# Mixed score bursts, five attention bursts a group, and two d_ff chunks side by side in a fused attention and feed-forward kernel

## Chip, cores and metric

The kernel runs on one core of a Trainium2 chip. The metric is device time in microseconds; the time shown for a kernel is the median of several runs. Beside these runs there is one profiled execution, from which every row in this text comes.

## What is computed

Two attention results are added and fed to a two-layer network (8 batches, 8 heads, 576 positions, 64 per head; model width 512, d_ff 2048):

```python
q_d = q.reshape(B, H, Sd, 4, D).mean(axis=3)          # and k_d, v_d: Sd = 144
out_d = softmax(scale * q_d @ k_d.T) @ v_d            # "down" attention
out_up = np.repeat(out_d, 4, axis=2)
mask = np.abs(pos[:, None] - pos[None, :]) < 4        # "local" attention
out_local = softmax(where(mask, scale * q @ k.T, -1e9)) @ v
x = (out_up + out_local).transpose(0, 2, 1, 3).reshape(4608, 512)
h = x @ w_in
return (h / (1 + exp(-1.702 * h))) @ w_out            # float32
```

## The kernel before

**Feed-forward.** The 4608 tokens are cut into 9 groups of 512. For a group, `mm1` forms 16 chunks of d_ff (128 rows each, four matmuls of 128x512 that accumulate over the model width, L691), and ScalarE's SiLU (L702) turns each chunk into one slice of `gT`. Then `mm2` multiplies `gT` by `w_out` for four blocks of 128 tokens, 16 matmuls each (L747), and a ScalarE copy and a DMA store each block (L732). Group g's first product needs `xT`, the attention result of batches g and g-1 (a batch has 576 tokens), with one tile `xT[hp]` for each pair of heads; matmul dmc of a chunk reads `xT[dmc]`.

**Attention is woven in by position.** While group g's dense matmuls run, the attention of batch g+1 is computed in short bursts between them. The order is written by hand: all engines run in the order in which the code issues to them. A position below 16 stands before that chunk of `mm1`; a position from 16 stands before matmul (position - 16) of `mm2`. `POS` is for groups 1 to 6, `POS_0` for group 0; groups 7 and 8 have no attention. The steps of `attention` in groups 1 to 6, with their old positions:

- 13: scores of the first four heads, `s_pe(0)`. `scores` issues 80 local matmuls (L367; 32 rows by 64 columns of the array, 60 columns streamed, ordered by segment i, half of the contraction a, column half par, row strip r). `scores_d` then issues 24 down matmuls (L386; 144 columns streamed).
- 16: `s_act(0)`: ScalarE loads the exponential's table and takes two local exponentials (L397) and the down one (L403); VectorE multiplies by the mask (L411).
- 33: the same for the other four heads, and the SiLU table is loaded again (L661).
- 42: attention times values of head pairs 0 and 1 (80 matmuls, L428 and L450); VectorE normalises (L466, L467).
- 53: the same for pairs 2 and 3.
- 62: transposes of pairs 0 and 1 (26 matmuls each, L481 and L491); ScalarE copies the down part fourfold (L605), VectorE adds it to the local part into `xT` (the merge, L626 and L632).
- 71: the same for pairs 2 and 3.

Group 0 has nine steps (its transposes one by one), with its bank pairs chosen by hand, and 14 further matmuls at 41 (L329) that reduce v.

**PSUM.** Eight banks: three pairs `PA[0..2]`, which attention takes in turn (`ps_tile`), and two single banks `PM`, which the chunks of `mm1` and the blocks of `mm2` take alternately. A score step takes three pairs (two local, one down), an attention step two, a transpose one. A matmul that writes into a bank waits until the last reader has finished. In group 0 the token blocks 2 and 3 (from position 32) go to `PA[0]`.

**Beside it**, at a group's start, VectorE transposes the next batch's q and k (L262), GpSimd reduces them and v (L292, L296, L308, L311) and issues loads, and SP issues loads of v and the stores.

Of the kernel before, what the change touches and what calls it, by code (L numbers as in the profile page):

```python
# [19 lines left out]
def kernel(  # L20
# [9 lines left out]
    nc = tc.nc  # L30
    B, H, S, D = q.shape
    SD = S // 4
# [3 lines left out]
    n_dmc = d_model // 128  # L36
# [3 lines left out]
    KSTART = (0, 56)  # L40
    QSTART = (0, 60)
# [314 lines left out]
    def scores(b, qd, barred=False, sp=None):  # L356
        sp = sp or [ps_tile(), ps_tile()]
        if barred:
            bar_others(sp)
        for i in range(5):  # L360
            for a in range(2):
                for par in range(2):
                    for r in range(4):
                        rows = slice(32 * r, 32 * r + 32)
                        k0 = 114 * i + KSTART[par]
                        q0 = 114 * i + QSTART[par]
                        nc.tensor.matmul(  # L367
                            sp[r // 2][64 * par : 64 * par + 64, r % 2, 60 * i : 60 * i + 60],
                            lhsT=kT[b, qd][rows, k0 : k0 + 64, a],
                            rhs=qT[b, qd][rows, q0 : q0 + 60, a],  # L370
                            start=(a == 0 and not barred),
                            stop=(a == 1 or barred),
                            tile_position=(32 * r, 64 * par),
                            skip_group_check=barred,
                        )
        return sp

    def scores_d(b, qd, sd=None):
        sd = sd or ps_tile()
        bank = banks(sd)  # L380
        for kc in range(3):
            for a in range(2):
                for r in range(4):
                    rows = slice(32 * r, 32 * r + 32)
                    j = r % 2
                    nc.tensor.matmul(  # L386
                        bank[r // 2][64 * j : 64 * j + 64, SD * kc : SD * kc + SD],
                        lhsT=kdT[qd][rows, 48 * kc : 48 * kc + 64, a],
                        rhs=qdT[b, qd][rows, :, a],
                        start=(a == 0), stop=(a == 1),  # L390
                        tile_position=(32 * r, 64 * j),
                    )
        return sd

    def exp_local(qd, sp):
        for u in range(2):
# [61 lines left out]
    def normalise(o):  # L458
        y = work.tile([128, 2, 7, D], BF16, name="y", tag="y", bufs=4)
        rc = work.tile([128, 2, 7, 1], FP32, name="rc", tag="rc")  # L460
        for xs in (slice(0, 1), slice(1, 2)) if o is PM else (slice(0, 2),):
            n = xs.stop - xs.start
            ov = (o[xs.start][:, None, :] if o is PM else o)[:, :, 0:455].rearrange(
                "p x (c e) -> p x c e", e=65
            )
            nc.vector.reciprocal(rc[:, xs], ov[:, :, :, 64:65])  # L466
            nc.vector.tensor_tensor(  # L467
                out=y[:, xs], in0=ov[:, :, :, 0:D],
                in1=rc[:, xs].to_broadcast([128, n, 7, D]), op=ALU.mult,
            )  # L470
        return y

    def transp(y, n=None):
        x = ps_tile(n)
        for i in range(5):
            for par in range(2):
                for j in range(2):
                    pos = j if par == 0 else 1 - j
                    c0 = 0 if (par == 1 or i == 0) else 3
                    c1 = 60 if (par == 0 or i == 4) else 57  # L480
                    nc.tensor.matmul(  # L481
                        x[64 * j : 64 * j + 64, par, 57 * i + c0 : 57 * i + c1],
                        lhsT=y[64 * pos : 64 * pos + 60, par, i, :],
                        rhs=ident(pos, 60, c0, c1),
                        start=True, stop=True,
                        tile_position=(64 * pos, 64 * j),
                    )
        for c2, xx in ((0, 0), (0, 1), (1, 0)):
            for j in range(2):
                pos = j if xx == 0 else 1 - j  # L490
                nc.tensor.matmul(  # L491
                    x[64 * j : 64 * j + 64, xx, 288 + 48 * c2 : 336 + 48 * c2],
                    lhsT=y[64 * pos : 64 * pos + 48, j, 5 + c2, :],
                    rhs=ident(pos, 48, 0, 48),
                    start=True, stop=True,
                    tile_position=(64 * pos, 64 * j),
                )
        return x
# [149 lines left out]
    def attention(b, slots=None):  # L648
        st = {}

        def s_pe(qd):
            st["s", qd] = scores(b, qd)
            st["d", qd] = scores_d(b, qd)

        def s_act(qd):
            if qd == 0:
                nc.scalar.preload_act_table_set("exp_and_others")
            exp_local(qd, st["s", qd])
            exp_down(qd, st["d", qd])
            if qd == 1:  # L660
                nc.scalar.preload_act_table_set("silu_and_others")  # L661
            mask_local(qd)

        def s1():
            s_pe(1)
            s_act(1)

        def avn(*hps):
            def f():
                for hp in hps:  # L670
                    st["o", hp] = av(b, hp, slots and slots[hp % 2])
# [12 lines left out]

        first = [lambda: s_pe(0), lambda: s_act(0), s1, avn(0, 1)]
        if b == 1:
            return first + [tr(0), tr(1), avn(2, 3), tr(2), tr(3)]
        return first + [avn(2, 3), tr(0, 1), tr(2, 3)]

    def hps_mm(g, ffc, dmc, acc):  # L690
        nc.tensor.matmul(  # L691
# [9 lines left out]
    def silu(gT, ffc, acc):  # L701
        nc.scalar.activation(  # L702
            out=gT[:, ffc, :], in_=acc, func=AF.Silu, scale=GELU_SCALE
        )
# [100 lines left out]
    end_psel()  # L805
    prep_1("k", 0, 0)
    prep_1("q", 0, 0)
    sp = scores(0, 0, barred=True, sp=PA[0:2])
    exp_local(0, sp)
    reduce_qk(0, 0, "k")  # L810
    prep_1("k", 0, 1)
# [2 lines left out]
    reduce_qk(0, 1, "k")  # L814
    reduce_qk(0, 1, "q")
    warm(10)
    sp = scores(0, 1, barred=True, sp=PA[0:2])
    exp_local(1, sp)
    exp_down(0, scores_d(0, 0, PA[2]))
    warm(4)  # L820
# [124 lines left out]
```

## Time and profile before

| what | value |
|---|---|
| time, median of 3 runs | 324.64 us (324.64, 322.55, 325.23) |
| profiled execution | 323.04 us, span 321.2 us |
| TensorE busy | 312.3 us, 97% of the span |
| granted TensorE clock | 1.000 |
| L747 + L691 into pm, share of the chain that ended last | 37% + 37% |
| group 3 by the chain (128.67 to 162.13) | 33.46 us, of which 128 dense matmuls of 0.216 us take 27.6 |

The span is the time from the first to the last instruction of the program on the core; the execution's time has a little more around it. A row of a timeline gives the start of a run of like instructions, the union of their durations, engine, line, operation, output and inputs, and the count. Matmuls are pipelined and their ends are modelled, so the distance between starts tells more than a duration. "issue" in a chain is time in which an engine waited for nothing that the profile shows.

### The profile page before, as it was taken

How to read it: one execution, taken by the hardware profiler on the slowest of the kernel's cores; microseconds unless marked ns; L12 is line 12 of the kernel's file. 1: busy time of each engine (PE TensorE's matmuls, PEld its weight loads, DVE VectorE, ACT ScalarE, POOL GpSimd, SP SyncE). 2: the span in 40 equal slices, each digit the busy share in tenths (PEclk: the TensorE clock that was granted, in tenths of full speed). 3: DMA queues.
4: the chain of work that ended last, by engine and by line, in shares of the span. 5: the costliest groups of instructions: out<-in, count | busy, mean ns of one | idle time of the engine just before them, and what ended most of it. 6: DMA issues, size and time to landing. Idle time of an engine off the chain costs nothing.

```text
span 321.2 us, 10997 instructions
## 1 busy us (share of the span) xinstructions
PE 312.3 (97%) x4927; PEld 157.6 (49%) x4927; DVE 134.0 (42%) x221; ACT 183.7 (57%) x314; POOL 139.3 (43%) x170
## 2 busy tenths in 40 slices
PE   6899999999999989999999999999999999999995
PEld 3565554445544445455545554555445544444444
DVE  6965326812773066605770478036811650000000
ACT  4465771767456663668365936583677466415611
POOL 8956950299009910794059604970296000000000
PEclk9999999999999999999999999999999999999999
DMA  7999999999519931796159815991360110020012
GB/s 121 128 206 207 170 149 216 183 248 209 132 68 198 201 97 67 168 215 147 66 147 205 177 40 147 200 203 49 109 106 2 70 67 2 0 98 33 2 62 68
DMA packets 64078, 40.02 MB, mean 125 GB/s; under 512 B 44064, under 2 KB 55456, under 8 KB 64032
## 3 DMA queue, kind: packets, MB, share of 16 engines
q1 hardware_dynamic: 44496, 24.32, 33.0%
q0 software_dynamic: 19392, 14.95, 31.9%
q8 instruction: 38, 0.62, 0.8%
q10 hardware_dynamic: 144, 0.07, 0.1%
q14 instruction: 8, 0.07, 0.1%
HBM read 44.83 MB, written 9.44 MB: 169 GB/s over the span
## 4 chain that ended last, share of the span: by engine, by line
PE 94%; DVE 2%; DMA 2%; issue 1%; POOL 0%; ACT 0%; POOLq 0%
PE pm L691 37%; PE pm L747 37%; PE pa L367 3%; PE pa L747 2%; PE pa L691 2%; PE pa L428 2%; PE pa L386 2%; PE pa L481 2%; DMA qb<-in_q_dram 2%; PE pa L450 2%; PE pm L762 1%; PE pm L644 1%; DVE qT L262 1%; PE pa L491 0%; PE pa L506 0%
## 5 line engine op out<-in xcount | busy, mean ns | idle before, releaser
L747 PE MATMUL pm<-w_out_bf,gT 128*128 128x512 bf16 x528 | 121.8, 380 | 0.3 <-issue 0.3
L691 PE MATMUL pm<-xT,w_in_bf 128*128 128x512 bf16 x544 | 121.1, 379 | 0.0
L702 ACT ACTIVATE gT<-pm 128x512 bf16<-128x512 f32 x136 | 81.0, 598 | 44.6 <-PE pm L691 44.6
L691 PEld LDWEIGHTS <-w_in_bf 128*128 128x128 bf16 x576 | 55.5, 98 | 66.9 <-issue 0.4
L747 PEld LDWEIGHTS <-gT 128*128 128x128 bf16 x560 | 51.4, 98 | 59.8 <-issue 1.0
L411 DVE TENSOR_TENSOR es<-es,mask 128x600 bf16<-128x600 bf16 x28 | 20.0, 730 | 88.8 <-ACT es L397 88.0
L292 POOL TENSOR_TENSOR pq<-kT 128x576 f32<-128x576 bf16 x14 | 16.2, 1159 | 90.0 <-DVE kT L262 90.0
L732 ACT ACTIVATE osb<-pm 128x512 f32<-128x512 f32 (+2 forms) x35 | 20.8, 594 | 40.4 <-PE pm L747 36.5
L605 ACT COPY od<-pa 128x384 f32<-128x384 f32 (+1 forms) x56 | 18.5, 412 | 32.2 <-DVE y L467 19.7
L467 DVE TENSOR_TENSOR y<-pa,rc 128x896 bf16<-128x896 f32 x28 | 30.6, 1092 | 1.0
L626 DVE TENSOR_TENSOR xT<-pa,od 128x570 bf16<-128x570 f32 x28 | 21.1, 753 | 11.4 <-ACT od L605 10.1
L734 DVE TENSOR_SCALAR osb<-pm 128x128 f32<-128x128 f32 x1 | 0.3, 292 | 55.3 <-ACT osb L732 55.3
L308 POOL TENSOR_TENSOR v<-v 112x512 f32<-112x512 f32 x18 | 22.8, 1266 | 0.0
L397 ACT ACTIVATE es<-pa 128x600 bf16<-128x600 f32 x32 | 19.7, 668 | 5.2 <-PE pa L367 5.0
L262 DVE STREAM_TRANSPOSE kT<-kb 128x576 f32<-128x576 f32 x16 | 20.0, 1249 | 3.5 <-DMA kb<-in_k_dram 3.4
L262 DVE STREAM_TRANSPOSE qT<-qb 128x576 f32<-128x576 f32 x16 | 19.9, 1241 | 0.4
L367 PEld LDWEIGHTS <-kT 32*64 32x64 bf16 x1280 | 11.7, 104 | 8.5 <-issue 6.4
L367 PE MATMUL pa<-qT,kT 32*64 32x60 bf16 x1280 | 13.6, 203 | 1.9 <-DVE qT L262 1.9
L216 POOL DMA_DIRECT2D vb<-in_v_dram x20 | 13.7, 698 | 3.0 <-DMA w_in_bf<-in_moe_w_in_dram 1.1
L292 POOL TENSOR_TENSOR pq<-qT 128x576 f32<-128x576 bf16 x13 | 14.9, 1146 | 0.0
L403 ACT ACTIVATE ed<-pa 128x864 bf16<-128x864 f32 x16 | 14.4, 898 | 0.1
L311 POOL TENSOR_TENSOR vd<-v 112x256 bf16<-112x256 f32 x18 | 13.7, 759 | 1.4
(92 smaller groups left out, 257.9 us busy)
## 6 DMA issues: line engine op xcount, KB each, us to landing
out_dram<-osb SPq DMA_DIRECT2D x35, 256.0 KB, 2.1
vf<-in_v_dram SPq DMA_DIRECT2D x60, 128.0 KB, 5.3
v<-in_v_dram SPq DMA_DIRECT2D x36, 192.0 KB, 5.1
kb<-in_k_dram POOLq DMA_DIRECT2D x16, 288.0 KB, 7.2
qb<-in_q_dram POOLq DMA_DIRECT2D x16, 288.0 KB, 8.3
w_in_bf<-in_moe_w_in_dram POOLq DMA_DIRECT2D x4, 512.0 KB, 9.1
w_out_bf<-in_moe_w_out_dram POOLq DMA_DIRECT2D x4, 512.0 KB, 12.6
vb<-in_v_dram POOLq DMA_DIRECT2D x20, 64.0 KB, 5.4
```

Of the source, the lines that this page charges most:

```text
L262: nc.vector.transpose(out=t32.rearrange("p (i c) -> p c i", c=18), in_=store[b, qd].bitcast(FP32).rearrange("p (c d) -> p c d", c=18),)
L292: nc.gpsimd.tensor_tensor(out=t1, in0=sv[:, :, 0:2, :], in1=sv[:, :, 2:4, :], op=ALU.add)
L308: eng.tensor_tensor(out=t1[0:112], in0=x[:, :, 0:2, :], in1=x[:, :, 2:4, :], op=ALU.add)
L367: nc.tensor.matmul(sp[r // 2][64 * par : 64 * par + 64, r % 2, 60 * i : 60 * i + 60], lhsT=kT[b, qd][rows, k0 : k0 + 64, a], rhs=qT[b, qd] ...
L397: nc.scalar.activation(out=es[2 * qd + u][:, :, 0:300], in_=sp[u][:, :, 0:300], func=AF.Exp, scale=inv_sqrt_d,)
L411: nc.vector.tensor_tensor(out=ev, in0=ev, in1=mask, op=ALU.mult)
L467: nc.vector.tensor_tensor(out=y[:, xs], in0=ov[:, :, :, 0:D], in1=rc[:, xs].to_broadcast([128, n, 7, D]), op=ALU.mult,)
L626: eng.tensor_tensor(out=sub(xT[hp], t0 + 3, (57, 2), (114, 5), (1, 57)), in0=sub(x, 3, (509, 2), (57, 5), (1, 57)), in1=sub(od, 3, (57, 2) ...
L691: nc.tensor.matmul(acc, lhsT=w_in_bf[:, dmc, ffc * 128 : (ffc + 1) * 128], rhs=xT[dmc][:, g * TG : g * TG + TG], start=(dmc == 0), stop=(d ...
L702: nc.scalar.activation(out=gT[:, ffc, :], in_=acc, func=AF.Silu, scale=GELU_SCALE)
L732: eng.activation(out=osb, in_=ap, func=AF.Copy, scale=1.0 / GELU_SCALE)
L747: nc.tensor.matmul(ops[t], lhsT=gT[:, ffc, t * 128 : (t + 1) * 128], rhs=w_out_bf[:, ffc, :], start=(ffc == 0), stop=(ffc == n_ffc - 1),)
```

## The change

Four things change.

1. In the attention of batches 1 to 7, `scores_mixed` takes the place of `scores` and `scores_d`: for segments 0 and 1 only locals, and for segments 2, 3, 4 four down matmuls ahead of each eight locals. Within the eight, strips alternate between the column halves. The starting score bursts of batch 0 keep their order.
2. In groups 1 to 6 the last three bursts become two: `av_tr` (attention of pairs 2 and 3 and the transpose of pair 0) and transposes of pairs 1, 2 and 3.
3. In groups 1 to 8 the first two d_ff chunks are computed side by side in a pair of `PA`, the matmuls alternating between its two banks, and the two SiLUs are issued after them.
4. Positions: `POS` goes from 13, 16, 33, 42, 53, 62, 71 to 13, 16, 35, 45, 56, 69. In `POS_0` the second score step goes from 27 to 30.

```diff
+    def score_d(b, qd, sd, kc, a, r):
+        rows, j = slice(32 * r, 32 * r + 32), r % 2
+        nc.tensor.matmul(
+            sd[64 * j : 64 * j + 64, r // 2, SD * kc : SD * kc + SD],
+            lhsT=kdT[qd][rows, 48 * kc : 48 * kc + 64, a],
+            rhs=qdT[b, qd][rows, :, a],
+            start=(a == 0), stop=(a == 1),
+            tile_position=(32 * r, 64 * j),
+        )
...
+    def scores_mixed(b, qd):
+        sp, sd = [ps_tile(), ps_tile()], ps_tile()
+        for i in range(5):
+            for a in range(2):
+                if i >= 2:
+                    for r in range(4):
+                        score_d(b, qd, sd, i - 2, a, r)
+                for x in (1, 0):
+                    for r in range(4):
+                        score(b, qd, sp, i, a, r % 2 if x == 0 else 1 - r % 2, r)
+        return sp, sd
...
         def s_pe(qd):
-            st["s", qd] = scores(b, qd)
-            st["d", qd] = scores_d(b, qd)
+            st["s", qd], st["d", qd] = scores_mixed(b, qd)
...
         first = [lambda: s_pe(0), lambda: s_act(0), s1, avn(0, 1)]
         if b == 1:
             return first + [tr(0), tr(1), avn(2, 3), tr(2), tr(3)]
-        return first + [avn(2, 3), tr(0, 1), tr(2, 3)]
+
+        def av_tr():
+            for hp in (2, 3):
+                st["o", hp] = av(b, hp)
+            st["x", 0] = transp(st["y", 0])
+            for hp in (2, 3):
+                st["y", hp] = normalise(st["o", hp])
+            merge(b, 0, st["x", 0], copy_od(st["x", 0]))
+
+        return first + [av_tr, tr(1, 2, 3)]
...
     def mm1(g, gT, steps, first=0):
+        if g:
+            two = PA[1 if g == 1 else turn["a"] % 3]
+            for dmc in range(n_dmc):
+                for ffc in range(2):
+                    hps_mm(g, ffc, dmc, two[:, ffc, :])
+            for ffc in range(2):
+                silu(gT, ffc, two[:, ffc, :])
+            first = 2
...
-    POS = [13, 16, 33, 42, 53, 62, 71]
-    POS_0 = [16, 18, 27, 46, 52, 56, 65, 71, 75]
+    POS = [13, 16, 35, 45, 56, 69]
+    POS_0 = [16, 18, 30, 46, 52, 56, 65, 71, 75]
```

`score` is the body of the old loop in `scores`; nothing is added, removed or resized among the instructions, only their order and their PSUM tiles change.

More of the change, by code (lines that the diff above doesn't have):

```diff
@@ L354, in bar_others, with score, scores @@
             )
[L356 to L359, printed above, removed]
+    def score(b, qd, sp, i, a, par, r, barred=False):
+        rows = slice(32 * r, 32 * r + 32)
+        k0 = 114 * i + KSTART[par]
+        q0 = 114 * i + QSTART[par]
+        nc.tensor.matmul(
+            sp[r // 2][64 * par : 64 * par + 64, r % 2, 60 * i : 60 * i + 60],
+            lhsT=kT[b, qd][rows, k0 : k0 + 64, a],
+            rhs=qT[b, qd][rows, q0 : q0 + 60, a],
+            start=(a == 0 and not barred),
+            stop=(a == 1 or barred),
+            tile_position=(32 * r, 64 * par),
+            skip_group_check=barred,
+        )
+    def score_d(b, qd, sd, kc, a, r):
+        rows, j = slice(32 * r, 32 * r + 32), r % 2
+        nc.tensor.matmul(
+            sd[64 * j : 64 * j + 64, r // 2, SD * kc : SD * kc + SD],
[3 more added lines that the diff above has]
+            tile_position=(32 * r, 64 * j),
+        )
+    def scores(b, qd, sp):
+        bar_others(sp)
         for i in range(5):
@@ L363, in scores, with scores_d @@
                     for r in range(4):
[L364 to L375, printed above, removed]
-        return sp
-    def scores_d(b, qd, sd=None):
-        sd = sd or ps_tile()
-        bank = banks(sd)
+                        score(b, qd, sp, i, a, par, r, barred=True)
+        return sp
+    def scores_d(b, qd, sd):
         for kc in range(3):
@@ L383, in scores_d @@
                 for r in range(4):
[L384 to L392, printed above, removed]
-        return sd
+                    score_d(b, qd, sd, kc, a, r)
+        return sd
+    def scores_mixed(b, qd):
[9 more added lines that the diff above has]
+        return sp, sd
     def exp_local(qd, sp):
@@ L807 @@
     prep_1("q", 0, 0)
-    sp = scores(0, 0, barred=True, sp=PA[0:2])
+    sp = scores(0, 0, PA[0:2])
     exp_local(0, sp)
@@ L816 @@
     warm(10)
-    sp = scores(0, 1, barred=True, sp=PA[0:2])
+    sp = scores(0, 1, PA[0:2])
     exp_local(1, sp)
```

## Prediction

> **What bounds the kernel now.** I read the busy shares first, then the chain of work that ended last, then TensorE's timeline, and ScalarE's and VectorE's timelines only where TensorE must wait for them.
>
> ```profile
> PE 312.3 (97%) x4927; PEld 157.6 (49%) x4927; DVE 134.0 (42%) x221; ACT 183.7 (57%) x314; POOL 139.3 (43%) x170
> ```
>
> TensorE is busy 97% of a 321.2 us span; the chain is 94% TensorE. So whatever shortens TensorE's own stream shortens the kernel, unless it brings a wait. The chain's row "262.65 13.81 PE pm L691 x64" gives the price of a dense matmul: 13.81 / 64 = 0.216 us. The two products need 1152 of them, and the change leaves their number alone. What it alters lies between them, in the attention bursts:
>
> ```profile
> 128.50 11.39 PE L691 MATMUL pm<-xT,w_in_bf 128*128 128x512 bf16 x52
> 139.82 0.84 PE L367 MATMUL pa<-qT,kT 32*64 32x60 bf16 x80
> 140.46 0.59 PE L386 MATMUL pa<-qdT,kdT 32*64 32x144 bf16 x24
> 140.98 2.77 PE L691 MATMUL pm<-xT,w_in_bf 128*128 128x512 bf16 x12
> ```
>
> Columns: start, union of modelled durations (they overlap the next row, so I use starts), instruction, count. 52 dense matmuls take 11.22 us, but the burst starts 11.32 after them: **0.10 us to enter a burst**. The 80 local scores issue in 140.46 - 139.82 = 0.64 us, 8 ns each. The 24 down-scores take 0.52 up to the next dense matmul: single records show them in fours, one four every 65 ns, because each streams 144 columns; the four themselves issue in 33 ns (8.3 ns apart), so issue idles half of that time. This is what mixing can fill.
>
> **The score bursts.** No row shows locals and down-scores mixed, so I bound it. Below: 104 matmuls at the 8.3 ns beat, 0.64 + 24 x 0.0083 = 0.84, then the way out of a burst that ends in locals:
>
> ```profile
> 8.66 0.83 PE L367 MATMUL pa<-qT,kT 32*64 32x60 bf16 x80 [1.92 <-DVE qT L262]
> 9.43 2.33 PE L644 MATMUL pm<-wz 128*128 128x512 bf16 x10
> ```
>
> 80 locals and the exit take 0.77, so the exit is 0.13: 0.97 in all, against 140.98 - 139.82 = 1.16. Above: nothing overlaps, each of the six groups of 4 + 8 matmuls takes 65 + 8 x 8.3 = 131 ns, which with the first 32 locals (0.26) and the exit is 1.18. Even then it costs no more than now, as each kind only takes what it takes alone. I take 0.97. The down-scores and the locals after them use other column halves of the same row strips, and the 14 vd matmuls (L329), whose halves also share rows, start in pairs 3 to 17 ns apart, one pair every 107 ns: two halves stream at once. In the attention matmuls a square of the array takes a new 64-column weight and a 65-column matmul every 32 ns, so weight loads hide under matmuls. A group of 12 issues in 100 ns; a square that does a down-score (65) and a local (about 30) needs 95. It fits, barely.
>
> A rule speaks against this: the Trainium skill, "TensorE: Matmul & The Clock Gate", Part 3 (The mechanism), says that a weight load overlaps a running matmul only where the row group differs. By it the local after a down-score would wait out its 60 ns stream, about 30 ns in each group of twelve, 0.18 per burst, and the gain would be gone. The 65 ns beat here, on which the next weight load starts 2 ns after the matmul before it on the same rows, doesn't agree with it.
>
> The first burst of a group saves 0.19. The second now takes 1.23 to 1.30 (mean 1.25), since a separate wait (EVENT_SEMAPHORE, x7, 51 ns) ahead of its down-scores leaves issue empty for 80 ns. The built program keeps that wait ahead of the first down-score, now after 32 locals, exactly where single records show a 97 ns refill gap anyway. Between 0.97 and 1.05 I take 1.01: 0.24 saved. 7 x 0.19 + 7 x 0.24 = **-3.0 us** (0 to -3.3).
>
> Does the down-score wait move to a worse place? It now comes 0.25 instead of 0.65 us into the burst and needs the exponential of the first pair's down-scores finished. In group 3 that ends 4.12 us after position 16 (147.71 against 143.59); the burst at 35 starts 4.2 after it and reaches the down-scores at 4.45. Covered.
>
> **Five bursts instead of six (groups 1 to 6).**
>
> ```profile
> 50.82 0.35 PE L481 MATMUL pa<-id,y 60*64 60x60 bf16 x20
> 50.99 0.22 PE L491 MATMUL pa<-id,y 48*64 48x48 bf16 x6
> 51.15 1.04 PE L747 MATMUL pm<-w_out_bf,gT 128*128 128x512 bf16 x4
> ...
> 153.99 0.35 PE L428 MATMUL pa<-vb,es 64*64 64x65 bf16 x20
> ...
> 154.81 2.12 PE L747 MATMUL pm<-w_out_bf,gT 128*128 128x512 bf16 x9
> ...
> 156.86 0.35 PE L481 MATMUL pa<-id,y 60*64 60x60 bf16 x20
> ...
> 157.41 2.12 PE L747 MATMUL pm<-w_out_bf,gT 128*128 128x512 bf16 x9
> ```
>
> One transpose of 26 matmuls takes 0.33 alone, two take 0.55: 0.22 for 26 more, 0.11 for leaving. Old: 0.82 + 0.55 + 0.55 = 1.92 and three entries. New: (0.82 + 0.22) + (0.55 + 0.22) = 1.81 and two. 0.11 + 0.10 = 0.21, times 6: **-1.26 us**.
>
> Its waits, from rows of group 3: the transpose of pair 0 takes the bank pair of output 1, so both normalises (0.24 + 1.09, pitch 1.3) must be over. They start about 0.55 into the burst at 45 and end 3.2 after its start; the transpose starts 0.1 + 0.82 + 2.37 + 0.1 + 0.7 = 4.1 after it. At 69, pair 3 reuses pair 0's banks: VectorE has normalise 2 and 3 and merge 0 (0.75 + 0.17) behind the burst at 56, done about 4.1 after its start, needed at 4.5. Then three copies (0.66 a pair) and three merges (0.87 each) feed the next group: the last ends 3.9 after the start of the burst at 69, and 11 dense matmuls plus six of the next group put the need at 4.6. All covered, by 0.4 us and more. The moved steps issue no DMA, so nothing stands behind them on POOL or SP; VectorE's next transposes start about 0.1 us later, with 10 us to the scores that need them.
>
> **First two chunks side by side.** It takes one wait away. In group 1, 52 matmuls (row at 59.94) take 11.56 instead of 11.39: the fourth waits for the last merge, released at 60.77. Now that input is needed at the seventh: **-0.17**. The bank pair that the chunks take was last read by merge 1 (done 2.2 after the burst at 69 starts, needed at 3.3). But it brings a wait of its own. Both SiLUs are issued after all eight matmuls, and in the built program the first waits for the eighth. From 128.50 and 129.57: SiLU starts 0.42 after its chunk's last matmul starts.
>
> ```profile
> 129.57 0.60 ACT L702 ACTIVATE gT<-pm 128x512 bf16<-128x512 f32 x1 [0.27 <-PE pm L691]
> ...
> 60.15 1.09 ACT L732 ACTIVATE osb<-pa 128x512 f32<-128x512 f32 x2 [0.42 <-PE pa L747]
> ```
>
> Two of this size back to back start 0.49 apart. So SiLU 0 starts 7 x 0.216 + 0.42 = 1.93 into the group, SiLU 1 at 2.42, SiLU 2 at 2.91, not 2.79; it ends at 3.51. Chunk 4 reuses chunk 2's bank at 16 x 0.216 = 3.45 and needs 0.05 more: 0.11 late, with all of TensorE behind it. Groups 1 to 8: **+0.9 us** (0.4 to 1.6).
>
> **Group 0: score burst from 27 to 30.** Here the third token block (position 32) writes into bank pair 0, which this burst's second pair of scores holds until its exponential ends.
>
> ```profile
> 42.14 0.84 PE L367 MATMUL pa<-qT,kT 32*64 32x60 bf16 x80
> 42.86 0.58 PE L386 MATMUL pa<-qdT,kdT 32*64 32x144 bf16 x24
> 43.37 1.25 PE L747 MATMUL pm<-w_out_bf,gT 128*128 128x512 bf16 x5
> 44.46 2.11 PE L747 MATMUL pa<-w_out_bf,gT 128*128 128x512 bf16 x9
> ```
>
> ```profile
> 43.03 1.23 ACT L397 ACTIVATE es<-pa 128x600 bf16<-128x600 f32 x2 [0.50 <-PE pa L367]
> ```
>
> Now the exponentials end at 44.26 and TensorE comes at 44.46: covered by 0.2. New: the burst starts 0.19 earlier for the first burst's gain, 0.65 later for three more matmuls: 42.60. Locals end with the burst, the last at 43.43; exponentials 0.26 later, over 1.23 after that: 44.92, 44.97 at TensorE. It arrives after two matmuls, at 42.60 + 0.97 + 0.43 = 44.00. **+0.97 us** (0.8 to 1.1).
>
> **Sum:** -3.0 - 1.26 - 0.17 + 0.9 + 0.97 = -2.6. The profiled execution took 323.04 (span 321.2 and 1.84 around it): 320.4. The three runs have 324.64 as median, 1.6 more; the four together average 323.87, so I give **321.3 us**, by its bounds 320.0 to 322.5.
>
> **Rivals.** (A) Mixing overlaps nothing (the rule above, or a short matmul that may not end before a long one ahead of it). For: no row shows the mix, and the fit is within 5 ns. Against: the beats above. 3.0 lost: 324.3; halfway 322.8.
>
> (B) The two new waits don't show, or TensorE stalls less for instructions. SiLU 2's lateness is a difference of tenths, and the chain has stalls that the change may shift:
>
> ```profile
> 116.84 0.90 issue
> 117.75 0.37 PE pa L450 x18
> ```
>
> Single records put them at TensorE's instructions 1985, 3009, 4033 and 7617, all 193 plus a multiple of 256, each ending 1.4 us after a packet of the instruction queue (38 of 16 KB): instructions that come late. Together 2.3 us in this execution. Without the new waits 319.4.
>
> (C) Slower: denser bursts outrun that fetch. The 4033 stall came where 256 instructions (a score burst, 9 dense matmuls, most of an attention burst) were wanted 3.6 us after the block before was begun, and arrived after 4.6. The new combined burst is 212 instructions long. If one block in each of groups 1 to 6 is late as that one was, 6 x 0.9 = 5.4: 326.7. It decides where a block is used up in less than about 4 us. Against: positions are spread by one to four matmuls (0.2 to 0.9 us), which gives the time back. The Trainium skill, "Runtime: NRT & Kernel Launch", Instruction fetch mechanics, calls such boundaries mostly hidden; the 0.90 above isn't.
>
> **Chances:** forecast 0.50, A 0.20, B 0.18, C 0.12. The range, 319.3 to 324.6, holds the first three. About 1% (3.2 us) is what a measurement here can tell from no change; the forecast lies near that edge, so it is split: faster 0.36, same 0.54, slower 0.10.
>
> **What would show it.** Score bursts of 0.97 to 1.05 from first score to next dense matmul (A: 1.15); two bursts of 1.04 and 0.77 where three stood; about 0.97 before L776 into pa near 44 us with the exponential as releaser; 0.1 before chunk 4 of each group; "issue" stalls of some 2 us. I am wrong if down-scores hold up locals, if merge 3 comes after the next group's seventh matmul, or if stalls for instructions move by more than 1 us.

## The result and the profile after

The changed kernel takes 321.87 us (median of 12 runs, 319.79 to 324.89) against 324.46 us for the kernel before (12 runs beside it, 322.55 to 325.23): a ratio of 0.9923, 95% interval 0.9901 to 0.9945. A second comparison of the same two kernels, 9 against 14 runs, gave 321.53 against 323.72, ratio 0.9915 (0.9884 to 0.9945). So 2.2 to 2.6 us went, 0.8%: clear of zero by the intervals, less than the 1% that the prediction named as the least difference to be told from no change, and 0.6 us from the forecast of 321.3. A ratio leaves out single runs that lie more than 1.5% above the fastest of their kernel (here the one of 324.89).

The profiled execution of the changed kernel took 322.29 us (span 320.5, granted clock 0.998), only 0.75 less than that of before. The difference to the medians is a first hint that single executions carry something that the kernel's text does not decide.

The first page of the changed kernel, busy time, share of the span and instructions by engine:

```profile
PE 309.9 (97%) x4927; PEld 156.8 (49%) x4927; DVE 131.5 (41%) x221; ACT 183.2 (57%) x314; POOL 140.5 (44%) x170
```

The same number of TensorE instructions, and TensorE busy for 2.4 us less: the bursts are shorter.

TensorE's timeline of the changed kernel, the last two bursts of group 3 and the first score burst of group 6 (start, union of durations, instruction, count):

```profile
154.84 0.35 PE L441 MATMUL pa<-vb,es 64*64 64x65 bf16 x20
...
155.71 0.23 PE L504 MATMUL pa<-id,y 48*64 48x48 bf16 x6
155.88 2.98 PE L776 MATMUL pm<-w_out_bf,gT 128*128 128x512 bf16 x13
158.79 0.35 PE L494 MATMUL pa<-id,y 60*64 60x60 bf16 x20
...
159.41 0.22 PE L504 MATMUL pa<-id,y 48*64 48x48 bf16 x6
159.57 2.55 PE L776 MATMUL pm<-w_out_bf,gT 128*128 128x512 bf16 x11
...
240.10 0.33 PE L360 MATMUL pa<-qT,kT 32*64 32x60 bf16 x32
240.34 0.27 PE L372 MATMUL pa<-qdT,kdT 32*64 32x144 bf16 x4
240.37 0.27 PE L360 MATMUL pa<-qT,kT 32*64 32x60 bf16 x8
...
240.90 0.26 PE L360 MATMUL pa<-qT,kT 32*64 32x60 bf16 x6
241.09 2.76 PE L712 MATMUL pm<-xT,w_in_bf 128*128 128x512 bf16 x12
```

Where three bursts stood, two take 155.88 - 154.84 = 1.04 and 159.57 - 158.79 = 0.78 us. In the score burst four down-scores are out after 0.03 us and eight locals follow at once, where one set of four down-scores took 0.065 before. From the first score to the next dense matmul it is 241.09 - 240.10 = 0.99; the kernel before took 1.16.

The chain of work that ended last in the changed kernel (start, length, what):

```profile
43.76 1.22 ACT es L410 x2
45.02 2.10 PE pa L776 x9
...
56.70 1.41 issue
...
117.91 0.98 issue
...
218.18 0.42 issue
```

The first two rows are the new wait of group 0: the matmul into `pa` stands behind the exponentials, and its start lies 1.20 us after the one before it, 0.99 more than the 0.216 of a dense matmul. The rows called "issue" are the stalls for late instructions; a row starts when the matmul before it has ended, so it is shorter than the stall. The chain of before has 0.90 us at the place near 117 us (the row stands in the prediction), no row near 218, and these two:

```profile
56.14 0.34 issue
...
86.24 0.24 issue
```

ScalarE's timeline of the changed kernel at the start of group 3, which begins at 128.91:

```profile
130.84 1.08 ACT L723 ACTIVATE gT<-pa 128x512 bf16<-128x512 f32 x2 [1.13 <-PE pa L712]
131.81 0.60 ACT L723 ACTIVATE gT<-pm 128x512 bf16<-128x512 f32 x1
132.56 0.60 ACT L723 ACTIVATE gT<-pm 128x512 bf16<-128x512 f32 x1 [0.15 <-PE pm L712]
```

The third SiLU starts 2.90 us into the group and ends at 3.50 (forecast 2.91 and 3.51). Chunk 4 starts 0.10 late there and in each of groups 1 to 7, 0.16 in group 8: 0.86 in all.

### The profile page after: what moved, and what is told of

Read it like the earlier page. It is cut to its first block, busy times and chain, and to the rows that moved or that the text cites. A ratio compares the mean times of both kernels' runs of the same rounds, so it can differ in the third digit from the quotient of the medians.

```text
span 320.5 us, 10996 instructions
## 1 busy us (share of the span) xinstructions
PE 309.9 (97%) x4927; PEld 156.8 (49%) x4927; DVE 131.5 (41%) x221; ACT 183.2 (57%) x314; POOL 140.5 (44%) x170
## 4 chain that ended last, share of the span: by engine, by line
PE 92%; DMA 4%; issue 1%; POOL 1%; ACT 1%; DVE 0%; POOLq 0%
PE pm L776 36%; PE pm L712 33%; PE pa L712 6%; PE pa L360 3%; PE pa L776 2%; PE pa L441 2%; DMA qb<-in_q_dram 2%; PE pa L494 2%; PE pa L372 2%; PE pa L463 2%; DMA vb<-in_v_dram 1%; PE pm L791 1%; PE pm L657 1%; PE pa L504 0%; ACT es L410 0%
## 5 line engine op out<-in xcount | busy, mean ns | idle before, releaser
L712 PE MATMUL pm<-xT,w_in_bf 128*128 128x512 bf16 x480 | 107.9, 379 | 0.0
L723 ACT ACTIVATE gT<-pm 128x512 bf16<-128x512 f32 x120 | 71.5, 599 | 37.4 <-PE pm L712 37.4
L424 DVE TENSOR_TENSOR es<-es,mask 128x600 bf16<-128x600 bf16 x28 | 17.7, 632 | 93.3 <-ACT es L410 92.0
L308 POOL TENSOR_TENSOR v<-v 112x512 f32<-112x512 f32 x18 | 24.0, 1331 | 0.0
L712 PE MATMUL pa<-xT,w_in_bf 128*128 128x512 bf16 x96 | 23.0, 379 | 0.0
L360 PE MATMUL pa<-qT,kT 32*64 32x60 bf16 x1280 | 17.1, 199 | 1.6 <-DVE qT L262 1.6
L360 PEld LDWEIGHTS <-kT 32*64 32x64 bf16 x1280 | 14.7, 104 | 8.1 <-issue 6.5
L723 ACT ACTIVATE gT<-pa 128x512 bf16<-128x512 f32 x24 | 13.2, 604 | 9.1 <-PE pa L712 9.1
```

Source lines behind the costliest of these rows:

```text
L308: eng.tensor_tensor(out=t1[0:112], in0=x[:, :, 0:2, :], in1=x[:, :, 2:4, :], op=ALU.add)
L360: nc.tensor.matmul(sp[r // 2][64 * par : 64 * par + 64, r % 2, 60 * i : 60 * i + 60], lhsT=kT[b, qd][rows, k0 : k0 + 64, a], rhs=qT[b, qd] ...
L712: nc.tensor.matmul(acc, lhsT=w_in_bf[:, dmc, ffc * 128 : (ffc + 1) * 128], rhs=xT[dmc][:, g * TG : g * TG + TG], start=(dmc == 0), stop=(d ...
L723: nc.scalar.activation(out=gT[:, ffc, :], in_=acc, func=AF.Silu, scale=GELU_SCALE)
```

## How the time was taken apart

Single records let TensorE's stream be cut in three for each kernel: the start up to the first score burst of group 0; the stalls at TensorE's instruction 193 of each 256 that last over 0.15 us (a stall is what a distance between starts has above the usual one); and the rest, from that burst to the last matmul without those stalls. The rest is what the kernel's own order decides, and the short pauses inside bursts that are told of below. All in us; "median" is of the timed runs beside their own runs of before.

| kernel | median | ratio to before, 95% | profiled execution | stalls in it | rest |
|---|---|---|---|---|---|
| before | 323.4 to 324.5 | 1 | 323.04 | 2.34 | 276.89 |
| changed | 321.87 | 0.9923 (0.9901 to 0.9945) | 322.29 | 3.52 | 274.95 |
| changed, again | 321.53 | 0.9915 (0.9884 to 0.9945) | 321.98 | 3.05 | 274.53 |
| two tiles for chunks 0, 1 | 321.35 | 0.9917 (0.9889 to 0.9945) | 321.48 | 2.79 | 274.37 |
| group 0 burst at 27, not mixed | 321.24 | 0.9919 (0.9892 to 0.9947) | 321.72 | 3.31 | 274.05 |
| both | 321.10 | 0.9912 (0.9878 to 0.9946) | 320.61 | 3.18 | 273.39 |
| chunks one by one | 322.35 | 0.9955 (0.9935 to 0.9975) | 322.76 | 2.80 | 275.61 |
| other order of the locals | 321.70 | 0.9952 (0.9926 to 0.9978) | 321.06 | 2.59 | 274.82 |
| mixing alone | 323.35 | 0.9986 (0.9960 to 1.0013) | 323.30 | 5.07 | 274.64 |
| all but the mixing | 322.72 | 0.9987 (0.9963 to 1.0010) | 322.14 | 0.88 | 276.88 |
| before, few loads | 322.14 | 0.9963 (0.9941 to 0.9985) | 322.19 | 0.35 | 276.78 |
| changed, few loads | 320.12 | 0.9895 (0.9860 to 0.9929) | 320.12 | 1.51 | 274.15 |
| both, few loads | 318.51 | 0.9852 (0.9811 to 0.9894) | 317.89 | 1.33 | 272.80 |

A shorter measure is the length of group 6, from the first matmul of its first product to that of group 7, which held none of these stalls: 33.40 us before, 32.85 changed, 32.97 with mixing alone, 33.26 with all but the mixing, 32.98 with the chunks one by one, 32.75 with two tiles.

## The experiments

### The two new waits

The changed kernel was timed once more beside three variants of it.

> The changed kernel once more, to compare the next three with on the same chip. Every theory: 321.9 us, ratio to the kernel before 0.992. The theory of the instruction blocks says one thing more: the stalls lie at the same instructions (TensorE's instruction 193 of each 256), but not with the same lengths, since the lengths differ from execution to execution: their sum was 2.3 us in the trace of before and 3.7 us in that of after, and another execution of after shows another sum, anywhere from 1.5 to 4.5 us.

321.53 us; the stalls were 0.70, 0.24, 0.65, 0.33 and 1.13 us, 3.05 in all, at the same instruction positions and with other lengths than the 1.57, 0.19, 1.16 and 0.60 of the first trace. As expected.

**Two tiles for the first two chunks.**

```diff
-            two = PA[1 if g == 1 else turn["a"] % 3]
+            t = turn["a"]
+            two = [PA[1][:, u, :] if g == 1 else PA[(t + u) % 3][:, 0, :] for u in range(2)]
...
-                    hps_mm(g, ffc, dmc, two[:, ffc, :])
-            for ffc in range(2):
-                silu(gT, ffc, two[:, ffc, :])
+                    hps_mm(g, ffc, dmc, two[ffc])
+                    if g > 1 and dmc == n_dmc - 1:
+                        silu(gT, ffc, two[ffc])
```

> The first two d_ff chunks of groups 2 to 8 write to two different PSUM tiles, and each chunk's SiLU is issued right after that chunk's last matmul. Theory of the tile: TensorE waits at chunk 4 because the SiLU of chunk 0 is released only when both chunks of the shared two-bank tile are written, which puts the two SiLUs behind one another. The wait, 0.10 us in each of groups 2 to 7 and 0.16 in group 8, goes, 6 x 0.10 + 0.16 = 0.76: 321.1 us against 321.9 for the changed kernel. Rival, ScalarE's rate: ScalarE is behind because it has two SiLUs and a block's copy to do in that stretch, whatever releases them; then the wait shows at chunk 4 or 5 as before, 321.9. The gap before chunk 4's first matmul is 0.216 us in groups 2 to 8 in the first case and 0.315 in the second.

The wait went where the edit reaches: group 6 takes 32.75 for 32.85, group 7 27.63 for 27.72, group 8 27.56 for 27.71, and group 1 keeps its 0.10. So it was the release of the first SiLU, not ScalarE's rate. The median moved by 0.18 us, less than the interval of either kernel; the 0.76 is shown in the trace, not in the times.

**The second score burst of group 0 back at 27, locals before down-scores.**

```diff
-            st["s", qd], st["d", qd] = scores_mixed(b, qd)
+            f = scores_split if b == qd == 1 else scores_mixed
+            st["s", qd], st["d", qd] = f(b, qd)
...
-    POS_0 = [16, 18, 30, 46, 52, 56, 65, 71, 75]
+    POS_0 = [16, 18, 27, 46, 52, 56, 65, 71, 75]
```

`scores_split` issues all locals, then all down-scores, into the same tiles.

> The second score burst of group 0 stands at position 27 again, local scores first and down-scores after them, as in the kernel before; all other bursts stay mixed. Theory of the position: the 0.99 us wait before the matmul into pa goes, the burst costs 1.32 in place of 1.08, so 0.99 - 0.24 = 0.75 less: 321.1 us against 321.9. Rival, the wait moves: the same stretch of ScalarE's exponentials holds up a later step of group 0 (the attention bursts at 46 and 52), and at most 0.2 is gained: 321.7. Second rival, instruction blocks: the wait covered part of a block's load, and the stall at TensorE's instruction 1985 (1.57 us in the trace of after, 0.49 in that of before) grows by what is saved: 321.9.

No wait is left before the matmul into `pa`. From its first score burst to group 1, without the stall at instruction 1985, group 0 takes 20.78 us for 21.52: 0.74 less, as the theory of the position has it. That stall was 0.96 us here, between the 1.57 and the 0.70 of the two traces of the changed kernel, so it did not take the gain by rule. The median moved by 0.29.

> Both edits together. If the two waits are all that the change paid for its gains, and nothing comes in their place: 0.76 + 0.75 = 1.5 less, 320.4 us against 321.9, ratio to the kernel before 0.9875. If the loads of instruction blocks set the pace behind these waits, less than 0.5 of it is seen: 321.4.

The rest fell by 1.14 to 1.56 against the two traces of the changed kernel, the median by 0.43. Neither expectation is met by the times: 321.10 lies between 320.4 and 321.4, and the interval of the ratio is more than 1 us to either side. What hid the gain was left to the runs with few loads below.

### The parts of the change

**Chunks one by one again** (`if g:` of the new block in `mm1` becomes `if False:`).

> The changed kernel with the first two d_ff chunks one after the other again, as in the kernel before; everything else as changed. Theory of the late merge: with five attention bursts the last merge ends later, and without the side-by-side chunks the fourth matmul of groups 1 to 7 waits for it, some 0.2 us each (estimate from the durations in the trace of before), 7 x 0.2 = 1.4; the waits at chunk 4, 0.86 in the trace of after, go: 321.9 + 1.4 - 0.86 = 322.4 us. Rival, the merge is in time: nothing waits at the fourth matmul, and only the 0.86 is gained: 321.0.

322.35, where the first theory has 322.4. The chain of this kernel shows the late merge ahead of group 7's fourth matmul (start, length, what):

```profile
261.84 0.77 DVE xT L639
262.85 7.93 PE pm L712 x36
```

VectorE's last merge ends (a short second part of 0.17 us follows the row shown) and TensorE goes on; by single records the fourth matmul comes 0.18 late in group 1, 0.19 in group 2 and 0.23 to 0.24 in groups 3 to 7. So the side-by-side chunks pay for themselves: they cost 0.10 a group and avoid 0.2.

**The other order of the locals.**

```diff
-                for x in (1, 0):
+                for x in (0, 1):
```

> The changed kernel with the two sets of four local scores in the other order, so that the four local scores that come right after four down-scores use the same rows and columns of the TensorE array as these do, one by one. Theory of the square: a score matmul is held by the one before it on the same 32 rows and 64 columns, which the trace of before shows as 65 ns per eight down-scores more than for local scores; then each of the six such meetings of a burst costs some 32 ns, 6 x 0.032 = 0.19 per burst, over fourteen bursts 2.7 us: 324.6. Rival, the issue beat: a pair of weight load and matmul takes 8.3 ns whatever array part the pair before it used, as long as four follow one another on four row groups: 321.9.

TensorE's timeline, first score burst of group 6 with this order:

```profile
238.88 0.33 PE L360 MATMUL pa<-qT,kT 32*64 32x60 bf16 x32
239.11 0.27 PE L372 MATMUL pa<-qdT,kdT 32*64 32x144 bf16 x4
239.18 0.24 PE L360 MATMUL pa<-qT,kT 32*64 32x60 bf16 x6
...
239.69 0.24 PE L360 MATMUL pa<-qT,kT 32*64 32x60 bf16 x8
239.86 2.76 PE L712 MATMUL pm<-xT,w_in_bf 128*128 128x512 bf16 x11
```

From the first score to the next dense matmul it is 0.98 us, against 0.99, and group 6 takes 32.85 in both. The local after a down-score now wants the same 32 rows and the same 64 columns, and it does wait: by single records it starts 63 ns after that down-score (the second and third row), where on the other column half it followed after 33 ns. But the weight loads go on meanwhile, one every 8.3 ns, and the matmuls behind make the wait up: each group of twelve takes some 100 ns in both orders, which is the issue of its twelve pairs. So the theory of the square is right about the hold and wrong about its price of 0.032 us a meeting: as long as a square gets through its own matmuls within that time, the beat of 8.3 ns a pair is what counts.

This bears on the rule that the prediction weighed. The Trainium skill, "TensorE: Matmul & The Clock Gate", Part 3 (The mechanism), lets a weight load overlap a running matmul only where the row group differs; by it (an estimate), both orders would have cost about 0.18 us a burst more than the 0.99 and 0.98 measured here. This case's traces don't agree with it: the first weight load after four down-scores starts 29 ns after the down-score on its rows, which by the 63 ns above is then still streaming.

**Mixing alone** (six attention bursts, chunks one by one, positions of before but 35 for the second score burst).

> Six attention bursts, chunks one after the other and the positions of the kernel before (the second score burst of groups 1 to 6 at 35, of group 0 at 27): mixing alone. Mixing by the bursts of after: seven first bursts 1.255 to 1.097, seven second ones 1.344 to 1.161, 2.4 us; in group 0 the mixed burst at 27 waits for ScalarE, some 0.19 for its first down-score and 0.28 before pa (estimates from durations in the trace of before), 0.47 against: 324.46 - 2.4 + 0.5 = 322.6 us. Rival: the five bursts and the chunks, not the mixing, brought the gain: 324.5 or more.

In group 6, 33.40 becomes 32.97: 0.43, the 0.19 + 0.24 of the prediction's step. In group 0 the waits at 27 were 0.38 before the first down-score and 0.34 before `pa`, 0.72 and not 0.47. The rest fell by 2.25 us, yet the median stands at 323.35, level with before. The chain says where it went:

```profile
56.22 0.40 issue
86.16 0.74 issue
116.79 1.09 issue
217.35 1.62 issue
```

By single records it is 5.07 us of stalls in this execution, whose time lay at the kernel's median, against 2.34 in that of before: in it the late instructions took the gain. Part of this is the kernel's own order. Between positions 35 and 42 stand seven dense matmuls where nine stood, and the 256 instructions ahead of the stall at 217 us are used up in 2.76 us, against 3.41 before.

**All but the mixing** (`s_pe` issues all locals, then all down-scores, in groups 0 to 6).

> The changed kernel with the down-scores behind the local scores again in groups 0 to 6: five bursts, the chunks side by side and the new positions without the mixing. If mixing is worth what the bursts of the trace show, 2.4 us are lost; in group 0 the exponential starts before the down-scores, so that some 0.5 of the 0.99 us wait before pa goes (estimate): 321.9 + 2.4 - 0.5 = 323.8 us. Rival: the rest of the change brought the gain, 321.4 to 321.9.

TensorE's timeline, the same burst of group 6, not mixed:

```profile
239.53 0.84 PE L360 MATMUL pa<-qT,kT 32*64 32x60 bf16 x80
240.16 0.59 PE L372 MATMUL pa<-qdT,kdT 32*64 32x144 bf16 x24
240.69 2.76 PE L721 MATMUL pm<-xT,w_in_bf 128*128 128x512 bf16 x11
```

1.16 again, and 33.26 for group 6, 0.41 above the changed kernel. The rest is 276.88, 1.93 to 2.35 above it, with 0.49 less of the wait in group 0: mixing is worth 2.4 to 2.8 us. The median, 322.72, is 1.1 under the 323.8 expected; the profiled execution, 0.58 below the median, stalled for only 0.88 us.

So the sums of the parts hold in the rest and fail in the medians, and what differs between the two are the stalls. The last four runs are about them.

### What the stalls are

In every trace they lie at TensorE's instruction 193 plus a multiple of 256, each ending 1.3 to 1.7 us after a 16 KB packet of the instruction queue. Two things could be changed without touching what TensorE does: the traffic beside those packets, and the place in the program at which a block ends.

```diff
     def load_1(name, src, store, b, qd):
+        if b > 2:
+            store[b, qd] = store[b - 2, qd]
+            return
...
     def load_v(b, gate=None, chunks=range(5)):
+        if b > 2:
+            vf[b] = vf[2]
+            return
...
     def load_v4(b):
+        if b > 2:
+            return
```

> The kernel before, with q, k and v loaded for the first three batch items only; the attention of the later ones reads the tensors of earlier ones again, so that their output is not the reference's, while every engine issues the same computing instructions. It takes some 17 MB of loads out of groups 1 to 5. Theory of the blocks: a block of 256 TensorE instructions comes by DMA, its load waits behind the loads of q, k and v, and where it arrives late TensorE stands still. Then the stalls of 0.42, 1.09 and 0.34 us at 86, 118 and 218 us of the trace of before go (under 0.3 us in all is left), the one at 56 us stays, as the loads of group 0 stay; the median falls by 1.5 to 2.5 us, to about 321.7 from 323.7. Rival: the stalls come from somewhere else, the instruction stream or the tensor program, and stay, 323.5.

The chain of the kernel before with few loads has one such row after its start phase:

```profile
57.26 0.19 issue
```

The stalls at 86, 118 and 218 us are gone, 0.35 us is left of 2.34, and the rest is the same (276.78, was 276.89). The median fell by 1.3 us, a little less than the 1.5 to 2.5 expected. The loads delay the blocks: shown, by the medians and by one trace.

> The changed kernel with the same loads left out. With the stalls out of the way the change shows at its own worth: by the stretches of the two traces without stalls, 276.5 us from the first score burst of group 0 to the end before and 274.3 after, 2.2 us, with some 0.2 more for shorter pauses in the bursts either way; so 2.0 to 2.7 us below the same kernel before without these loads, some 319.3. If denser bursts outrun the instruction blocks (the rival with 326.7 of the prediction, at a smaller size), the stalls take part of the gain in the full kernels only, and the difference here is larger than the 2.6 us between the full kernels' medians, 3 us or more.

320.12 (319.34 to 320.81) against 322.14 (321.51 to 323.44): 2.02 us, no overlap between the two sets. The rest fell by 2.63, which is the prediction's sum, but 1.16 of stalls came on top (0.45 of it in group 0, whose loads stay), and the start, which differs by 0.6 between the two executions, makes up the difference. The chain of this kernel:

```profile
57.24 0.64 issue
...
216.14 0.28 issue
```

With no loads in groups 2 and 5, blocks are still late at 117 and 216 us, by 0.24 and 0.46, where the kernel before had none. Denser bursts explain little of it. Call the moment at which TensorE reaches instruction 193 of a 256 a boundary; the packet of the block that is needed at one boundary starts near the boundary before. By single records:

| boundary, kernel (few loads) | 256 instructions used up in | packet starts after the boundary before | packet takes | stall |
|---|---|---|---|---|
| 117 us, before | 3.51 us | 1.06 | 1.06 | none |
| 117 us, changed | 3.41 | 0.96 | 1.43 | 0.24 |
| 217 us, before | 3.41 | 0.73 | 0.95 | none |
| 216 us, changed | 3.40 | 0.99 | 1.61 | 0.46 |

Half a mixed score burst lies ahead of 117 us, and 0.10 us is what it brings; ahead of 216 us the stream is as dense as before. The rest is packets that took longer or came later, in one execution of each kernel; whether the change makes them so is open. So of the 0.7 us for two blocks at most 0.10 is shown to be the prediction's slower rival, and the expectation for it, a difference of 3 us or more with the loads gone, was not met.

The pauses inside the bursts go with the loads too. The chain's rows of the second score burst in group 3, first locals and next dense matmuls, for the changed kernel with all loads and with few:

```profile
148.23 0.26 PE pa L360 x31
...
149.35 2.27 PE pm L776 x10
...
146.66 0.26 PE pa L368 x31
147.64 2.26 PE pm L784 x10
```

1.12 and 0.98 us from row to row. With all loads, issue pauses for 0.13 to 0.15 us in four of the fourteen bursts of the changed kernel's first trace, and one to six times, for 0.10 to 0.16, in each other trace with mixed bursts, always in groups 1 to 5, whose loads are left out here. With few loads no mixed burst pauses: the 14 of this kernel take 0.98 to 0.99 us each, as do the 13 mixed ones of the next. Against the 1.163 and 1.240 (means of first and second bursts) of the kernel before with few loads, that is 7 x 0.177 + 7 x 0.253 = 3.0 us, the prediction's term. How a load holds up issue is not shown.

> The changed kernel with both waits taken out (two tiles for the first two chunks, the second score burst of group 0 as before at 27) and the same loads left out. The two edits are worth 1.3 us by the stretches without stalls (274.3 to 273.0), but their medians in the full kernels moved by 0.2 to 0.4. If the scatter of the stalls, 2.4 to 5 us from execution to execution, covers them, the 1.3 shows here: 318.0 us. If something else took the gain back, the difference is under 0.5: 319.

318.51 (317.27 to 320.09), 1.61 below the changed kernel with few loads; the rest fell by 1.35. With the loads out of the way the two edits show in the times, though the two sets of six overlap by 0.75 us. This fits stalls that covered them in the full kernels. How much of a gain the stalls take for good is not settled: from one trace each, scaled to the median, the changed kernel stalls for some 2.6 to 3.1 us and the one with both edits for 3.7 (estimates: the profiled execution's stalls, corrected by its distance from the median).

**128 instructions further.**

```diff
-    warm(21, 336)
+    warm(53, 133)
...
-    warm(10)
+    warm(40, 128)
...
-    warm(4)
+    warm(6, 341)
```

> The changed kernel with both waits taken out and 64 more pairs of weight load and matmul in the idle start (the same filler work cut in narrower pieces), so that every later TensorE instruction stands 128 places further in the stream. Theory of the blocks: the stalls stay at instruction 193 of each 256, and so hit other instructions of the program: in the attention bursts of groups 2 and 5, where the stall of 118 us lies at the 57th matmul and that of 218 us at the 47th, it moves 64 pairs ahead, out of the burst to the dense matmuls before it, or to the burst before; the time is that of the kernel without the shift, 321.1, give or take 1.5 for the stalls. Rival: the stall belongs to the burst, and stays at the same matmuls.

The chain of the shifted kernel:

```profile
12.44 1.94 issue
...
19.55 1.02 issue
...
47.08 2.68 issue
...
191.60 1.17 issue
```

All four end at instruction 193 of a 256 (449, 705, 1473 and 6593). In groups 2 and 5 nothing stalls: the boundaries now fall on a dense matmul at 123 us and on a score burst at 223 us, each reached 1.9 us after its block was there. The stall belongs to the block, not to the burst. The time was 327.79 (4 runs, 319.08 to 328.65), 6.7 above what was expected. In the profiled execution 4.3 us of this lie in the start. The shorter filler matmuls use up the first full block in 3.65 us, against 4.49 in the kernel with both edits, and its packet starts 0.65 us later; the two stalls there last 1.94 and 1.02 us for 0.71 and 0.22 (by the chains), and after each of them TensorE's clock was granted at half for 3.4 us. The stall of 2.7 us in the middle of group 0's second score burst had the same sequel. Windows of this kernel (us, then busy time and instructions of TensorE, weight loads, VectorE, ScalarE and GpSimd, granted clock, DMA share, GB/s):

```profile
46.00:50.00 4.00, 1.32 (x85) 0.78 (x85) 0.68 (x2) 1.05 (x2) 0.00 (x0) 0.88 1.20 206
50.00:56.00 6.00, 6.00 (x65) 2.52 (x48) 0.94 (x2) 3.30 (x4) 0.18 (x1) 0.51 1.14 219
56.00:60.00 4.00, 4.00 (x105) 2.22 (x104) 0.77 (x2) 0.80 (x1) 0.00 (x0) 1.00 0.90 180
```

From 49.05 to 55.88 us the granted clock is 0.50, and after the burst a dense matmul takes 0.425 us for 0.216. One late block cost 2.7 us and then about 2.5 more. One of the four executions, the one of 319.08, kept a clock of 0.999 and is 2.0 us faster than the kernel without the shift; the other three had 0.979 to 0.984. So the place of the stalls is settled by this run, and the cost of the shift is not.

## Why the prediction was right

The forecast, 321.3 us with a sum of -2.6, met 321.87 and a difference of 2.2 to 2.6. Point by point:

- **Score bursts, -3.0.** Right in an undisturbed group: 0.43 in group 6, mixing alone, and 0.41 when it is taken out; a clean burst takes 0.99 for the 0.97 forecast, and with few loads all fourteen together save the 3.0. The reason given, that a square's down-score and local fit into the issue of a group of twelve, is what single records show. With all loads it was 2.4 in the first trace (0.16 a first burst, 0.18 a second on average): of the seven second bursts three took 0.99 and four 1.12 to 1.14 for the 1.01 taken for all, because issue pauses somewhere after the 61st to the 94th matmul (over all traces). The prediction had no term for these pauses; they go when the loads go, and what a load does to issue stays open.
- **Five bursts, -1.26.** Right: 1.04 and 0.78, three entries become two, 0.21 a group, and none of the waits that the prediction called covered showed.
- **Group 1's wait, -0.17.** Right, and more was behind it: without the side-by-side chunks that wait stands in all seven groups, 0.18 to 0.24 each. The prediction had not priced this, as it took the chunks and the five bursts one by one.
- **SiLU wait, +0.9.** 0.86, by the mechanism described; two tiles take it away.
- **Group 0, +0.97.** 0.99, with the exponential as releaser.
- **Sum.** As measured in the first trace the terms give -2.4 - 1.26 - 0.17 + 0.86 + 0.99 = -2.0, and its rest fell by 1.94 (276.89 to 274.95); with few loads the score bursts give -3.0 and the sum -2.6, and the rest fell by 2.63 (276.78 to 274.15). So the sum is right for the kernel's own order when nothing disturbs it. With all loads it is some 0.6 too large, and that the medians of the first comparison still differ by 2.6 is partly luck of the stalls.
- **Readings.** Two are a little off and enter no sum: the block ahead of the stall at 118 us was wanted after 3.51 us, not 3.6, and the vd pairs start every 110 to 113 ns, not 107.

Rival A, no overlap, is refuted by two kernels (1.16 unmixed, 0.99 mixed in either order). Rival B had two conditions: the waits do show, and the stalls became no fewer. Rival C, denser bursts outrun the blocks, was priced at one late block in each of six groups, 5.4 us, deciding below 4 us a block. What the runs showed in its place: there is no one such point. With few loads blocks used up in 3.2 us are in time, where their packet starts 0.6 us before the boundary, and two that are used up in 3.4 are late by 0.7 together, at most 0.10 of it by denser bursts. The rival shows best in mixing alone, whose mixed burst and nearer positions use up a block 0.65 us sooner than in the kernel before. In the profiled execution of the changed kernel the stalls grew by 1.2 us, past the 1 us that the prediction named as a sign of being wrong, and turned the 1.94 of the rest into 0.75; over many executions they did not. The stalls of before, 2.3 us in its trace, were likewise a draw: its median lies 0.4 to 1.4 above that execution.

The Trainium skill, "Runtime: NRT & Kernel Launch", Instruction fetch mechanics, describes blocks of 256 instructions fetched while the current one runs, at a cost that is mostly hidden. The blocks are as the traces have them; the cost in these traces was 0.9 to 5.1 us an execution with the loads in place.

The kernel with both edits is the fastest in its own stretches (rest 273.39) and by its median of 321.10, but cannot be told from the changed kernel by its times.

## What to carry to other kernels

Small matmuls on different row strips are paid by their issue as long as each square of the array gets through its own streaming in that time, so put the ones that stream long between the ones that stream short, and check after each such gain which wait it has moved closer: here an exponential (0.99 us in all) and a merge (1.5 us where the chunks go one by one). Where small matmuls stand close together, compare the time in which 256 instructions are used up with the time at which the next block comes; a gain that shortens such a stretch may be taken back by a stall. And when the profiled execution and the medians disagree by the size of the change, take the known random part out of the trace before judging the parts, and take its source out of the kernel before judging by time.

## What was not expected of the hardware

- With few loads, the blocks for which TensorE had to wait in groups 1 to 6 came 3.6 to 4.0 us after the boundary before (the packet starts 0.9 to 1.1 us after it, takes 1.2 to 1.6, and the instructions follow 1.3 to 1.5 later), but other packets started up to 2.4 us before that boundary. With all loads the packet of a late block started up to 4 us after it, from group 0's first score burst on.
- In the trace of the shifted kernel the granted clock fell to 0.50 three times, for 3.4, 3.4 and 6.8 us, each time at or after a stall (1.94, 1.02 and 2.68 us by the chain). In the other traces it did not, with single stalls of up to 1.8 us from group 0's first score burst on. That the stall is what halves it is not tested.
- Issue inside a mixed burst pauses for 0.10 to 0.16 us in some bursts of groups 1 to 5, and in none when the loads are left out.
- Each score burst has a gap of 95 to 100 ns after its 32nd matmul, in the kernel before, in the changed one and with the other order of the locals.
- A separate semaphore wait ahead of a down-score cost 0.08 us of issue in the burst of before, and nothing where it falls on that gap.
